# The last pair's second layer as three word passes, with the words made between the groups of the first layer

## The chip, the cores and the metric

One core of one Trainium2 chip runs the kernel. TensorE (PE) multiplies matrices; its weight loads are shown as PEld. VectorE (DVE), ScalarE (ACT) and GpSimd (POOL) do the elementwise work, and SyncE (SP) issues nearly all DMAs. Each engine executes its own instructions in program order and waits for others through semaphores. Here the order of the program is the order in which the Python code emits instructions: the kernel switches the scheduler off (`tc.manual_schedule()`). The metric is the device time of one execution in microseconds (us), as the median of several runs.

## The reference

First a state-space scan (Mamba-2), then a two-layer network with an ELU between its layers. In short:

```python
# attention part: x (4, 8, 768, 32), a (4, 8, 768), B and C (4, 8, 768, 16)
cum = cumsum(log(a))                  # in chunks of tokens
M = (C @ B.T) * exp(cum_i - cum_j) * causal
y = M @ x + (C @ state) * exp(cum)    # and the state is carried on from chunk to chunk
# bridge: y -> 3072 tokens x 256
h = y @ w_in                          # 256 x 2048
g = where(h > 0, h, exp(min(h, 0)) - 1)
out = g @ w_out                       # 2048 x 256
```

All values are float32, and the output has 3072 rows of 256.

## The kernel before

The 3072 tokens are twelve blocks of 256. The blocks 0 and 1 go one by one; from block 2 on they go in pairs (n, n+1), so that n = 2, 4, 6, 8, 10 names a pair of 512 tokens. While the first layer of pair n runs, the scan of pair n + 2 and the second layer of pair n - 2 are threaded in between.

**First layer of a pair.** `l1_words(n, m)` computes one of sixteen groups m of 128 hidden units for 512 tokens. It uses *words*: a float32 number of 24 bits is split exactly into a high and a low word of 12 bits each, in the type `float32r`, which TensorE multiplies in one pass and without error for words this short. With w = w1 + w0 and y = WORD y1 - y0 three products are enough instead of four: `high` = w1 y1 + w0 y0, and `both` = (w0 + w1 / WORD)(y1 - y0); then w y = WORD both + (WORD - 1) high. So each group is three passes of two matmuls of 512 columns (L806), a scaled copy of `both` on ACT (L812), and the sum in place on DVE (L818). `begin_end` follows with two ACT instructions (L824 and L825, the exponential), and `end_words`, called in the middle of the next group, ends the ELU on DVE (L832) and writes the tile `g_of[n, m]`. For even m it also subtracts one half of the tile from the other on POOL (`sub`, L867, called on L836), which the second layer needs.

**Second layer of a pair.** `second(n)` multiplies blocks by the Strassen-Winograd scheme: token blocks, halves of the hidden units and halves of the output columns make a 2 x 2 x 2 product, which seven block products compute instead of eight. They run in two halves of the hidden units, and each product is four steps of two full float32 matmuls of 128 columns (L927). Sums of the weights (`w_sum`, and one quarter of `w_out` overwritten in place, L723), quarters of g that are subtracted from each other on POOL (`sum_t2`, and the calls of `sub` after the products 0 and 1), and additions of the results on DVE (L904, L979) belong to it. `second` is a generator: the loop over groups calls `l2s(count)`, which emits so many of its 56 steps after each group. For the last pair (n = 10) nothing remains to thread it into: `second(n, True)` runs alone at the end (L1376), stores what is complete early and computes its last product in two parts (L907 to L919).

**Buffers.** PSUM has seven buffers in the pool `ps_a` (`high`, `both`, the scan's results and every other product of `second`) and one in `ps_o`. In SBUF, `conv` holds the words of w_in (tag `w64`, eleven buffers) and `ffn` the tiles of g. `raw` and `att` hold what the scan needs; it ends inside the groups of pair 8.

**Order around the change.** The loop `for n in range(4, NP, 2)` (L1327) emits for each of sixteen groups: `l1_words`, a part of the scan's preparation, `begin_end`, the stores of pair n - 4 (at k = 0) and some steps of `second(n - 2)`. The one queue of SP takes the loads of the scan, the stores and, early on, the loads of the weights. `w_out` is ready when POOL has added its last words (L248), before the steps j = 4 and later of the loop on L1196 finish.

Of the kernel before, what the change touches and what calls it, by code (L numbers as in the profile page):

```python
# [10 lines left out]
F32 = mybir.dt.float32  # L11
# [21 lines left out]
def kernel(  # L33
# [38 lines left out]
    assert NG == 3 and MC == 16 and KC == 2 and CW == DM  # L72

    const = ctx.enter_context(tc.tile_pool(name="const", bufs=1))
    raw = ctx.enter_context(tc.tile_pool(name="raw", bufs=3))
    att = ctx.enter_context(tc.tile_pool(name="att", bufs=2))
    ffn = ctx.enter_context(tc.tile_pool(name="ffn", bufs=2))
    conv = ctx.enter_context(tc.tile_pool(name="conv", bufs=2))
    PSUM = bass.MemoryType.PSUM
    p_a = ctx.enter_context(tc.tile_pool(name="ps_a", bufs=7, space=PSUM))  # L80
    p_o = ctx.enter_context(tc.tile_pool(name="ps_o", bufs=1, space=PSUM))
# [647 lines left out]
    w_parts = w_out.rearrange("p (i k) (r c) -> p k r i c", k=2, c=P)  # L729
    a_out = [w_parts[:, k, r] for r in range(2) for k in range(2)]  # L730
    s_out = []

# [60 lines left out]
    def l1_words(n, m, ahead=None):  # L795


        cols = slice(m % 2 * P, (m % 2 + 1) * P)
        w, w0 = k_words[m // 2]
        w1, both_w, w0 = w[:, 0, :, cols], w[:, 1, :, cols], w0[:, :, cols]  # L800
        y1, y0, both_y = y_words[n]
        high, both = psum([P, 2 * BLK], "ps_h"), psum([P, 2 * BLK], "ps_w")
        passes = [(high, w1, y1), (high, w0, y0), (both, both_w, both_y)]
        for ps, lhs, rhs in passes if n > 2 and m == 0 else passes[2:] + passes[:2]:
            for k in range(KC):
                nc.tensor.matmul(  # L806
                    out=ps, lhsT=lhs[:, k], rhs=rhs[:, k], start=k == 0 and lhs is not w0,
                    stop=k == KC - 1 and lhs is not w1)
        if ahead:
            high_of_y(ahead)  # L810
        e = ffn.tile([P, 2 * BLK], F32, tag="e", name="e", bufs=2)
        nc.scalar.activation(e, both, ACT.Copy, scale=WORD)  # L812
        if late:
            end_words()
        if ahead:
            low_of_y(ahead)
            both_of_y(ahead)
        nc.vector.scalar_tensor_tensor(  # L818
            out=high, in0=high, scalar=WORD - 1.0, in1=e, op0=ALU.mult, op1=ALU.add)
        late.append((n, m, high, e))  # L820

    def begin_end():
# [6 lines left out]
    def end_words():  # L829
        n, m, h, e = late.pop(0)  # L830
        g_of[n, m] = ffn.tile([P, 2, BLK], F32, tag=f"g{m % 2}", name="g", bufs=12)
        nc.vector.scalar_tensor_tensor(  # L832
            out=g_of[n, m].rearrange("p b i -> p (b i)"), in0=e, scalar=1.0, in1=h,
            op0=ALU.subtract, op1=ALU.max)
        if m % 2 == 0 and (n, m) != (2, 14):
            sub(g_of[n, m][:, 1], g_of[n, m][:, 1], g_of[n, m][:, 0])  # L836

    def row_of(n):
# [48 lines left out]

    c_of = {}

    def second(n, last=False):  # L890


        c = c_of[n] = ffn.tile([P, 2, 2, 2, P], F32, tag="c", name="c_sum", bufs=1)
        c11, c12, c21, c22 = (c[:, at, :, e] for e in range(2) for at in range(2))
        a11, a12, s1, a22 = a_out
        s2, s3, s4 = s_out
        for half in range(2):
            if not half:
                tmp = ffn.tile([P, 3, 2, P], F32, tag="tmp", name="p_sum", bufs=1)
                p1, p5, u = (tmp[:, r] for r in range(3))  # L900
            chunk = range(4 * half, 4 * half + 4)

            def add(out, in0, in1, eng=nc.vector):
                eng.tensor_tensor(out=out, in0=in0, in1=in1, op=ALU.add)  # L904

            for r, a in enumerate((a11, a12, s1, s2, s3, a22, s4)):
                if last and half and r == 6:  # L907
                    store(n, 0)
                    for ts, queue in enumerate((nc.scalar, nc.sync)):
                        ps = psum([P, P], "ps_o")  # L910
                        for i in chunk:
                            nc.tensor.matmul(
                                out=ps, lhsT=quarters(n, i)[3][:, ts * P:(ts + 1) * P],
                                rhs=a[:, i], start=(i == chunk[0]), stop=(i == chunk[-1]))
                        nc.vector.tensor_tensor(
                            out=c12[:, ts], in0=ps, in1=c12[:, ts], op=ALU.add)
                        r0 = row_of(n + 1) + ts * P
                        queue.dma_start(out=out[r0:r0 + P, 0:P], in_=c12[:, ts])
                    return  # L919
                pool, tag = (p_a, "a") if (7 * half + r) % 2 or n == 2 and not half + r else (  # L920
                    p_o, "o")
                ps = pool.tile([P, 2, P], F32, tag=tag, name="ps_o")
                for i in chunk:
                    b11, b21, b12, b22 = quarters(n, i)
                    b = (b11, b21, b12, t2_of[n, i], b11, b21, b22)[r]
                    for ts in range(2):
                        nc.tensor.matmul(  # L927
                            out=ps[:, ts], lhsT=b[:, ts * P:(ts + 1) * P], rhs=a[:, i],
                            start=(i == chunk[0] and ts == 0), stop=(i == chunk[-1]),
                            skip_group_check=True)  # L930
                    if i < chunk[-1]:
                        yield
                if r == 0:
                    if half:
                        add(p5, ps, c22)
                        add(c21, ps, c21)
                        add(c11, ps, c11)
                    else:
                        nc.scalar.copy(out=p1, in_=ps)  # L939
                    for i in chunk:  # L940
                        b11 = quarters(n, i)[0]
                        sub(b11, t2_of[n, i], b11)
                elif r == 1:
                    add(c11, ps, c11 if half else p1)
                    for i in chunk:
                        b21 = quarters(n, i)[1]
                        sub(b21, b21, t2_of[n, i])
                elif r == 2:
                    add(p5, ps, p5 if half else p1)
                elif r == 3:  # L950
                    add(p5, ps, p5)
                    if half:
                        add(c12, c12, p5, nc.gpsimd)
                        add(c21, ps, c21)
                    else:
                        add(u, ps, p1)
                elif r == 4:
                    if half:
                        add(c21, ps, c21)
                    else:  # L960
                        add(u, ps, u)
                    add(c22, ps, p5)
                    if not half:
                        nc.scalar.copy(out=c12, in_=ps)
                    if last and half:
                        r0 = row_of(n + 1)
                        nc.sync.dma_start(
                            out=out[r0:r0 + BLK, P:2 * P].rearrange("(t p) c -> p t c", p=P),
                            in_=c22)
                    if not half:  # L970
                        sum_t2(n, 1)
                    elif n + 2 < NP:
                        sum_t2(n + 2, 0)
                elif r == 5:
                    add(c21, ps, c21 if half else u)
                elif half:
                    add(c12, ps, c12)
                else:
                    nc.vector.tensor_tensor(out=c12, in0=ps, in1=c12, op=ALU.subtract)  # L979
                yield  # L980

    def store(n, at):
        r0 = row_of(n + at)
# [212 lines left out]
    for j in range(2 * DIRECT):  # L1196
# [35 lines left out]
        if j == 4:  # L1232
            words_of_y(2)
            w_take(15, nc.vector)
            w_give(15)
        if j == 5:
            words_of_w(4)
            both_of_y(2)
# [88 lines left out]
    for n in range(4, NP, 2):  # L1327
# [6 lines left out]

        if n == 4:
            l2s(2)
        for k in range(16):
            l1_words(n, k, m if k == 15 else None)
            turn_step(n, k // 2 * 2 + 1, k % 2)
            if n == 4 and k == 0:  # L1340
                decay(6, 1)
            if n == 4 and 1 < k < 5:
                for _ in range(2):
                    next(left)()
# [5 lines left out]
                store(n - 4, 1)  # L1350
            if not m:
                l2s(4 if k % 2 else 3)
                continue
            l2s((3 - (n == 4), 3 - (n == 4), 3, 3, 3, 3, 3, 3, 4, 5, 2, 2, 3, 1, 3, 0)[k])
            if k == 9:
# [13 lines left out]
                inside(y, m, m + 1, t=1)  # L1369
        if m:  # L1370
            l2s(4)
        end_words()
        for _ in steps:
            pass
    n = NP - 2
    for k, _ in enumerate(second(n, True)):  # L1376
        if k == 0:
            store(n - 2, 0)
            store(n - 2, 1)


# [28 lines left out]
```

## Time and profile before

| | |
|---|---|
| median of 3 runs | 350.15 us (349.76 to 350.74) |
| span of the profiled execution | 347.9 us (the page gives no other time of that execution) |
| PE busy | 340.7 us (98%) |
| DVE, ACT, POOL busy | 258.4, 234.1, 218.0 us |
| chain that ended last | PE 63%, DVE 11%, ACT 10%, POOL 7% |
| granted TensorE clock | 0.999 of full speed |
| DMA in the slices of the last third | 0 to 1 tenths, 2 tenths in the last slice |

The span runs from the first to the last instruction of the program; the runs' times are longer by what lies around it. The chain is followed back from the last instruction: each piece is what the next one waited for. A timeline line gives the start, the duration, the engine, the line of the code, the operation, output and inputs, the shape, and how many instructions were merged; in brackets it has the idle time before it and who ended it. Matmuls overlap in such lines, so the price of one is the distance between starts. A full float32 matmul appears as two records.

### The profile page before, as it was taken

The numbers are of one execution on the slowest core, as the hardware profiler recorded it, in microseconds if no ns is written. First come the engines' busy times: TensorE is split into PE (matmuls) and PEld (weight loads), VectorE is DVE, ScalarE is ACT, GpSimd is POOL, SyncE is SP. The second block draws the span as 40 slices with busy tenths as digits, with TensorE's granted clock in tenths as the row PEclk, the third lists the DMA queues.
The fourth block names the chain that finished last, engine by engine and source line by source line (L and its number), as shares of the span: only waits on it lengthen the run. The fifth ranks groups of instructions, "written<-read, shape, count | busy, mean of one in ns | idle before, by whom it ended". The sixth has DMA issues, their size and how long they took to land.

```text
span 347.9 us, 9991 instructions
## 1 busy us (share of the span) xinstructions
PE 340.7 (98%) x3934; PEld 299.3 (86%) x3934; DVE 258.4 (74%) x515; ACT 234.1 (67%) x537; POOL 218.0 (63%) x338
## 2 busy tenths in 40 slices
PE   8899999999999999999999999999999999999996
PEld 6579888888788889889889888889988989999996
DVE  3998989889997899876788766778776756665232
ACT  4789989598658988457699457599557366565000
POOL 5654554539999799965296765196855174455760
PEclk9999999999999999999999999999999999999999
DMA  8989969381360610260421160320000100001002
GB/s 144 258 204 220 273 130 266 81 150 44 66 138 2 135 38 12 34 137 4 117 51 30 17 154 4 95 44 0 2 2 5 60 2 1 0 2 55 9 2 62
DMA packets 72728, 26.51 MB, mean 76 GB/s; under 512 B 57768, under 2 KB 67560, under 8 KB 72680
## 3 DMA queue, kind: packets, MB, share of 16 engines
q1 hardware_dynamic: 70360, 25.60, 31.7%
q8 instruction: 31, 0.51, 0.6%
q10 hardware_dynamic: 2320, 0.26, 0.5%
q14 instruction: 17, 0.14, 0.1%
HBM read 22.51 MB, written 3.34 MB: 74 GB/s over the span
## 4 chain that ended last, share of the span: by engine, by line
PE 63%; DVE 11%; ACT 10%; POOL 7%; issue 4%; SPq 2%; DMA 2%; DVEq 0%; POOLq 0%; ACTq 0%
PE ps_o L927 22%; PE ps_h L806 11%; PE ps_h L676 11%; PE ps_o L851 8%; PE ps_w L806 6%; DVE ps_h L818 3%; ACT e L824 3%; POOL g L867 3%; ACT e L825 2%; DMA w<-in_moe_w_in_dram 2%; POOL t L867 2%; DVE M L559 2%; PE ps_y L643 2%; DVE y L780 2%; POOL w L867 1%
## 5 line engine op out<-in xcount | busy, mean ns | idle before, releaser
L927 PEld LDWEIGHTS ps_o<-w_out,g 128*128 128x128 f32 x640 | 78.7, 191 | 5.4 <-ACT p_sum L939 1.2
L927 PE MATMUL ps_o<-w_out,g 128*128 128x128 f32 x640 | 81.2, 276 | 0.7 <-ACT p_sum L939 0.6
L824 ACT ACTIVATE e<-ps_h 128x512 f32<-128x512 f32 x72 | 43.0, 598 | 56.9 <-DVE ps_h L818 56.9
L832 DVE SCALAR_TENSOR_TENSOR g<-e,ps_h 128x512 f32<-128x512 f32 x72 | 49.4, 686 | 35.0 <-ACT e L825 33.4
L867 POOL TENSOR_TENSOR g<-g 128x256 f32<-128x256 f32 x36 | 28.6, 794 | 58.2 <-DVE g L832 58.2
L818 DVE SCALAR_TENSOR_TENSOR ps_h<-ps_h,e 128x512 f32<-128x512 f32 x72 | 50.0, 694 | 11.2 <-ACT e L812 9.0
L806 PE MATMUL ps_w<-y_both,w_words 128*128 128x512 f32 x144 | 51.5, 437 | 0.1
L812 ACT ACTIVATE e<-ps_w 128x512 f32<-128x512 f32 x72 | 42.2, 586 | 11.1 <-PE ps_w L806 11.0
L825 ACT ACTIVATE e<-e 128x512 f32<-128x512 f32 x72 | 45.5, 631 | 2.3
L676 PE MATMUL ps_h<-yT,w_in 128*128 128x256 f32 (+1 forms) x208 | 45.1, 367 | 1.9 <-ACT w_in L205 1.1
L806 PE MATMUL ps_h<-y,w_words 128*128 128x512 f32 x144 | 45.5, 398 | 0.0
L806 PE MATMUL ps_h<-y,w 128*128 128x512 f32 x144 | 44.9, 392 | 0.0
L676 PEld LDWEIGHTS ps_h<-yT,w_in 128*128 128x128 f32 x208 | 36.4, 190 | 7.5 <-POOL w_in L248 2.6
L530 ACT ACTIVATE L<-L,ncum 128x64 f32<-128x64 f32 x160 | 42.2, 337 | 0.1
L927 PE MATMUL ps_o<-w_sum,g 128*128 128x128 f32 x304 | 38.6, 276 | 0.0
L927 PEld LDWEIGHTS ps_o<-w_sum,g 128*128 128x128 f32 x304 | 37.0, 192 | 1.4
L535 POOL TENSOR_SCALAR_AFFINE_SELECT L<-L 64x512 f32<-64x512 f32 x40 | 29.4, 735 | 8.0 <-ACT L L530 6.7
L806 PEld LDWEIGHTS ps_h<-y,w 128*128 128x128 f32 x144 | 27.0, 188 | 6.9 <-POOL w L867 0.4
L806 PEld LDWEIGHTS ps_h<-y,w_words 128*128 128x128 f32 x144 | 26.6, 188 | 6.2 <-issue 0.5
L867 POOL TENSOR_TENSOR g<-t,g 128x256 f32<-128x256 f32 x40 | 28.1, 736 | 5.8 <-PE ps_o L927 5.7
L851 PE MATMUL ps_o<-w_out,g 128*128 128x256 f32 x128 | 30.4, 381 | 0.0
L867 POOL TENSOR_TENSOR g<-g,t 128x256 f32<-128x256 f32 x40 | 28.7, 748 | 0.2
(135 smaller groups left out, 537.5 us busy)
## 6 DMA issues: line engine op xcount, KB each, us to landing
L<-flat SPq DMA_DIRECT2D x20, 256.0 KB
w<-in_moe_w_out_dram SPq DMA_DIRECT2D x8, 512.0 KB
w<-in_moe_w_in_dram SPq DMA_DIRECT2D x7, 512.0 KB
xr<-in_x_dram SPq DMA_DIRECT2D x24, 128.0 KB
out_dram<-c_sum SPq DMA_DIRECT2D x9, 256.0 KB
bc<-in_B_dram SPq DMA_DIRECT2D x24, 64.0 KB
bc<-in_C_dram SPq DMA_DIRECT2D x22, 64.0 KB
ec<-flat_exp SPq DMA_DIRECT2D x10, 128.0 KB
```

The costliest lines, as they stand in the source:

```text
L530: nc.scalar.activation(L[:, h, u], L[:, h, u], ACT.Exp, bias=ncum[:, u, row:row + 1])
L535: nc.gpsimd.affine_select(out=part, in_=part, pattern=[[0, 4], [0, 2], [1, Q]], compare_op=ALU.is_ge, fill=0.0, base=0, channel_multiplier=-1)
L676: nc.tensor.matmul(out=ps[:, j, toks], lhsT=w_in[i][:, k, j * P:(j + 1) * P], rhs=yT[n // 2][:, k, n % 2].rearrange("p u i -> p (u i)")[:, ...
L806: nc.tensor.matmul(out=ps, lhsT=lhs[:, k], rhs=rhs[:, k], start=k == 0 and lhs is not w0, stop=k == KC - 1 and lhs is not w1)
L812: nc.scalar.activation(e, both, ACT.Copy, scale=WORD)
L818: nc.vector.scalar_tensor_tensor(out=high, in0=high, scalar=WORD - 1.0, in1=e, op0=ALU.mult, op1=ALU.add)
L824: nc.scalar.activation(e, high, ACT.Relu, scale=-1.0)
L825: nc.scalar.activation(e, e, ACT.Exp, scale=-1.0)
L832: nc.vector.scalar_tensor_tensor(out=g_of[n, m].rearrange("p b i -> p (b i)"), in0=e, scalar=1.0, in1=h, op0=ALU.subtract, op1=ALU.max)
L851: nc.tensor.matmul(out=o_of[n][:, ts], lhsT=g_of[n, j][:, m % 2, ts * P:(ts + 1) * P], rhs=w_out[:, m], start=(m == 0 and ts == 0), stop=( ...
L867: nc.gpsimd.tensor_tensor(out=out, in0=in0, in1=in1, op=ALU.subtract)
L927: nc.tensor.matmul(out=ps[:, ts], lhsT=b[:, ts * P:(ts + 1) * P], rhs=a[:, i], start=(i == chunk[0] and ts == 0), stop=(i == chunk[-1]), s ...
```

## The change

The second layer of the last pair no longer uses the seven block products. It is computed as sixteen contractions over 128 hidden units, for four blocks of 128 tokens, each in three word passes of 256 columns.

- `w_out` has to be had unchanged, since the scheme of the other pairs overwrites a quarter of it. `keep_w` copies its four quarters to a DRAM tile `w_kept`, one at j = 4 of the early loop, and three among the groups of n = 4.
- After the groups of n = 8 `late_pool` closes the pools of the scan and opens a pool in their place. Four DMAs bring the weights back, and buffers for their words are made.
- The words are *jobs*: eight for two slices of the weights each, sixteen for the tiles of g. A job has three steps: the high word on ACT, a second word on DVE, a third on POOL. From the third group of n = 10 on, `first_of_job` puts one ACT step behind the copy of `both`, `second_of_job` one DVE step behind L818, and `third_of_job` one POOL step behind the steps of `second(8)`, each for another job, so that a job passes through three groups. Jobs that are left (one of the weights, the last nine of g and the rest of those begun) go on beside the new second layer, and there the third step of g's words is on DVE too.
- `late_l2(m, t)` issues the three matmuls of slice m and token block t, `late_out` the copy on ACT, the sum on DVE and the store of a block. The first twelve slices go over all four token blocks each; the last four slices go block by block, so that the blocks end one after the other. The fourth block's `high` has its own PSUM bank.
- What the seven products needed goes: the subtractions of `end_words` and `sum_t2` for the last pair, and the special end of `second`.

```diff
-    def second(n, last=False):
+    def second(n):
...
-                if last and half and r == 6:
...
-                    elif n + 2 < NP:
+                    elif n + 4 < NP:
                         sum_t2(n + 2, 0)
...
+    def keep_w(k, r):
+        nc.sync.dma_start(out=kept_parts[:, k, r], in_=w_parts[:, k, r])
...
         nc.scalar.activation(e, both, ACT.Copy, scale=WORD)
+        if n == NP - 2 and m > 1:
+            first_of_job()
...
             out=high, in0=high, scalar=WORD - 1.0, in1=e, op0=ALU.mult, op1=ALU.add)
+        if n == NP - 2 and m > 1:
+            second_of_job()
...
-        if m % 2 == 0 and (n, m) != (2, 14):
+        if m % 2 == 0 and (n, m) != (2, 14) and n < NP - 2:
             sub(g_of[n, m][:, 1], g_of[n, m][:, 1], g_of[n, m][:, 0])
...
+    def late_words_of_w(i):
+        w, w1, both = late_w[i]
+        yield nc.scalar.activation(w1, w, ACT.Copy, scale=NEAR)
+        yield nc.vector.scalar_tensor_tensor(
+            out=both, in0=w1.bitcast(F32), scalar=1.0 / WORD - 1.0, in1=w,
+            op0=ALU.mult, op1=ALU.add)
+        yield sub(w.bitcast(F32R), w, w1.bitcast(F32))
+
+    def late_words_of_g(n, m):
...
+        yield nc.scalar.activation(words[:, 0], g, ACT.Copy, scale=NEAR / WORD)
+        yield nc.vector.scalar_tensor_tensor(
+            out=low, in0=words[:, 0].bitcast(F32), scalar=WORD, in1=g,
+            op0=ALU.mult, op1=ALU.subtract)
+        if alone:
+            yield nc.vector.scalar_tensor_tensor(
+                out=words[:, 1], in0=words[:, 0].bitcast(F32), scalar=1.0 - WORD, in1=g,
+                op0=ALU.mult, op1=ALU.add)
+        else:
+            yield sub(words[:, 1], words[:, 0].bitcast(F32), low.bitcast(F32))
...
+    def late_l2(m, t):
+
+        g1, g0, both_g = (g[:, t * P:(t + 1) * P] for g in late_g[m])
+        w0, w1, both_w = (w[:, m % 2] for w in late_w[m // 2])
...
+        if m == 0:
+            both = psum([P, 2, DM], "ps_both")
+            total.append((both[:, 0], psum([P, DM], "ps_high") if t == 3 else both[:, 1]))
+        both, high = total[t]
+        for ps, lhs, rhs in ((both, both_g, both_w), (high, g1, w1), (high, g0, w0)):
+            nc.tensor.matmul(
+                out=ps, lhsT=lhs, rhs=rhs,
...
+    def late_out(n, t):
+        both, high = total[t]
+        e = ffn.tile([P, DM], F32, tag="t2", name="e_out", bufs=4)
+        nc.scalar.activation(e, both, ACT.Copy, scale=WORD)
+        o = ffn.tile([P, DM], F32, tag="t2", name="o_out", bufs=4)
+        nc.vector.scalar_tensor_tensor(
+            out=o, in0=high, scalar=WORD - 1.0, in1=e, op0=ALU.mult, op1=ALU.add)
+        r0 = row_of(n + t // 2) + t % 2 * P
+        nc.sync.dma_start(out=out[r0:r0 + P, :], in_=o)
...
+            if n == 4 and k in (3, 5, 7):
+                keep_w(int(k > 3), int(k > 5))
...
                 l2s(4 if k % 2 else 3)
+                third_of_job()
                 continue
...
+        if m == NP - 2:
+            late_pool()
...
-    for k, _ in enumerate(second(n, True)):
-        if k == 0:
-            store(n - 2, 0)
-            store(n - 2, 1)
+    store(n - 2, 0)
+    store(n - 2, 1)
+    alone.append(True)
+    for m in range(MC - 4):
+        first_of_job()
+        second_of_job()
+        third_of_job()
+        for t in range(4):
+            late_l2(m, t)
+    for t in range(4):
+        for m in range(MC - 4, MC):
+            late_l2(m, t)
+        late_out(n, t)
```

## The prediction

> **What bounds the kernel now.** I read the page first: busy time, then the chain that ended last.
>
> ```profile
> PE 340.7 (98%) x3934; PEld 299.3 (86%) x3934; DVE 258.4 (74%) x515; ACT 234.1 (67%) x537; POOL 218.0 (63%) x338
> ...
> PE 63%; DVE 11%; ACT 10%; POOL 7%; issue 4%; SPq 2%; DMA 2%; DVEq 0%; POOLq 0%; ACTq 0%
> ```
>
> TensorE (PE) is busy 98%, and no other engine comes close. The chain in order of time then shows the stage that the change replaces:
>
> ```profile
> 317.95 25.01 PE ps_o L927 x224
> 342.96 1.80 PE ps_o L912 x16
> 344.76 0.02 issue
> 344.79 0.29 DVE c_sum L915
> ```
>
> At the end PE alone sets the time. These are 240 records of 0.1117 us. The first 16 belong to the pair before (its last product), so the last pair's second layer starts at 317.95 + 16 x 0.1117 = 319.74 and takes 224 x 0.1117 = 25.02, to 344.76. After that come 3.15 us of adding, storing and landing, to 347.91.
>
> What one matmul costs is read from PE's timeline, as the distance from start to start (the printed durations overlap):
>
> ```profile
> 107.49 0.62 PE L806 MATMUL ps_h<-y,w 128*128 128x512 f32 x2
> 107.95 0.62 PE L806 MATMUL ps_w<-y_both,w_words 128*128 128x512 f32 x2
> 108.41 0.62 PE L806 MATMUL ps_h<-y,w_words 128*128 128x512 f32 x2
> 108.86 0.61 PE L806 MATMUL ps_h<-y,w 128*128 128x512 f32 x2
> 109.31 3.61 PE L851 MATMUL ps_o<-w_out,g 128*128 128x256 f32 x16
> 112.76 1.05 PE L927 MATMUL ps_o<-w_out,g 128*128 128x128 f32 x8
> ...
> 319.57 5.52 PE L927 MATMUL ps_o<-w_out,g 128*128 128x128 f32 x48
> 324.93 1.95 PE L927 MATMUL ps_o<-w_sum,t 128*128 128x128 f32 x16
> ```
>
> A full f32 product is two records: 256 columns cost (112.76 - 109.31) / 16 = 0.216 per record, 128 columns (324.93 - 319.57) / 48 = 0.1117. A word product (L806) is one record: 512 columns in 0.45 to 0.47 per two, so 0.227 to 0.235 each.
>
> Last, the first layer's groups, where the new work is put. One group of the last pair, ScalarE (ACT) and VectorE (DVE):
>
> ```profile
> 305.44 0.58 ACT L812 ACTIVATE e<-ps_w 128x512 f32<-128x512 f32 x1
> 306.99 0.60 ACT L824 ACTIVATE e<-ps_h 128x512 f32<-128x512 f32 x1 [0.97 <-DVE ps_h L818]
> ...
> 306.26 0.70 DVE L818 SCALAR_TENSOR_TENSOR ps_h<-ps_h,e 128x512 f32<-128x512 f32 x1
> 307.08 0.42 DVE L904 TENSOR_TENSOR p_sum<-ps_o,p_sum 128x256 f32<-128x256 f32 x1
> 308.36 0.69 DVE L832 SCALAR_TENSOR_TENSOR g<-e,ps_h 128x512 f32<-128x512 f32 x1 [0.85 <-ACT e L825]
> 309.42 0.70 DVE L818 SCALAR_TENSOR_TENSOR ps_h<-ps_h,e 128x512 f32<-128x512 f32 x1 [0.38 <-PE ps_h L806]
> ```
>
> ACT waits 0.97 for L818, DVE 0.85 for the exponential and 0.38 for PE: here lies the free time that the words must fit into. A group lasts 2.7 (three steps of the layer before) or 3.2 us (four), 2.95 on average.
>
> **The last stage on PE.** Removed: 224 records, 25.02 us. Added: 16 x 4 x 3 = 192 word products of 256 columns. No row has that shape with words. Lower end: each needs a new 128x128 weight load, and the shortest step with one, 128 columns of f32, takes 0.112. Half of the 512-column word step is 0.116. If a word step shrinks with its columns as the f32 record does (0.216 to 0.1117), it is 0.231 x 0.517 = 0.120. If what a word step has above the f32 record, 0.231 - 0.216 = 0.015, is paid per instruction, it is 0.108 + 0.015 = 0.123. Upper end: if load and stream shared one read rate, (512 + 128) columns in 0.231 make (256 + 128) take 0.139. I take 0.120, the reading that rests on a measured halving: 192 x 0.120 = 23.0 us, a gain of 2.0 (3.5 at 0.112, a loss of 1.7 at 0.139).
>
> The Trainium skill (TensorE: Matmul & The Clock Gate, Back-to-back issue gap) gives N/2.4 + 2.5 ns for a warm matmul. For 512 columns that is 215.8; the word rows do not agree (227 to 235). By it the 192 would take an estimated 21.0 us.
>
> **The tail.** Now PE's end is followed by an add of 0.29 on 128x128 and a 64 KB store. Then: an ACT copy of 128x256 (0.37, row L939), whose input is complete two matmuls before PE ends, so 0.24 of it is covered; a VectorE operation on 128x256 (0.42, row L904); a 128 KB store. VectorE ends 0.05 + 0.37 - 0.24 + 0.42 = 0.6 after PE instead of 0.33: +0.27. A 256 KB store's packets of 1 KB take about 1.0 us, so 128 KB about 0.4 to 0.5 against 0.34: +0.1. Together +0.35 (0.2 to 0.8). The last copy also reuses the buffer of the first of the four stores, which by then has some 3 us, against 2.4 from issue to span end now: covered, by little.
>
> **Words in the first layer's groups.** From the third group on, one job each: an ACT copy (0.6), a VectorE operation on 128x512, and two groups after the copy a POOL subtraction of 128x512 (two rows of 0.735: 1.47). ACT: 0.6 goes into the wait of 0.97. POOL: the last pair's own subtractions go (8 of 0.74 in `end_words`, 4 after L972); some 12 x 1.47 = 18 come, beside 20 x 0.735 that stay, in 44 us. The t2, b11 and b21 quarters stand in the same queue; a subtraction ahead of them delays them by 1.5 to 4 us, and after the ninth group PE needs them 9 to 12 us later. Nothing. VectorE is the doubtful one: L818 and L832 start to start 0.61 each, 19 adds over 16 groups of 0.34 = 0.40, so 1.62 before; the job adds 0.61 alone, or more when POOL is reading:
>
> ```profile
> L780 DVE SCALAR_TENSOR_TENSOR y<-y,yT x10: 684/689/1216, 75.0 to 269.8; 128x512 fp32r<-128x512 f32 x10
> ...
> 269.35 1.11 POOL L867 TENSOR_TENSOR g<-g 128x256 f32<-128x256 f32 x1 [3.03 <-DVE g L832]
> ```
>
> With two SBUF inputs VectorE took 1.216 beside a POOL subtraction, 0.684 without; POOL took 1.11 instead of 0.735. L818 and L832 (one input in PSUM) never exceed 0.70. So 2.2 to 2.85 us per group, under 2.95. What lags is caught by PSUM: seven buffers at some 2.44 per group leave PE about 4 us. What can come out is the last `high` tile, which the fourth token block's sums take over: PE reaches it 9 matmuls (1.1 us) into the stage, and L832 has freed it 320.88 - 319.74 = 1.14 after the start now. I charge 0.3 (0 to 2.7, the rival below).
>
> The Trainium skill (SBUF — State Buffer, section SBUF: two separate sides) has this as an exclusive lock for the whole instruction, the loser blocked. The 1.216 agrees; by it a job behind a 1.47 us subtraction could last an estimated 2.1, and the sum would be the VectorE rival's.
>
> **The rest, charged nothing.** VectorE words after the first layer: 21 operations of 0.61 = 12.8 us beside 12 x 12 x 0.120 = 17.3 us of PE, no POOL behind them: the last one has 3 us in hand. The copy of the weights to DRAM (4 x 512 KB): the first DMA waits on SP for POOL's L248, which ends at 79.5; SP's next, a store at 83.5, is not held, and the first overwrite on POOL (L723, 92.7) comes 13 us later. The other three stand on SP ahead of loads needed a stage later. Lower end 0, upper end 0.6, one DMA issue on SP. The reload (4 x 512 KB) waits on SP for the scan's last product (264.3); at 200 to 270 GB/s (the page's slices) it is in by 275, before the third group (277). Behind it on SP stand the stores of the pair before, issued at 273.2 as now; VectorE first overwrites that tile at 281.1. If the reload took 16 us instead, VectorE would wait about 2 us, inside PE's 4.
>
> **Sum.** 347.91 - 25.02 + 23.04 + 0.35 + 0.3 = 346.6 us of span, 1.3 less. The page gives no time of the profiled execution beyond its span; the runs' median lies 2.24 above it (350.15), which I take as unchanged: 348.8 us.
>
> **Rivals.**
> Weights as the only limit (faster): steps of 0.112. For it: f32 rows with as many loads run at 0.112; against it: every word step exceeds the f32 record of the same page by 0.011 to 0.019. 21.5 us, so 347.3; the skill's rule would land beside it.
> Load and stream share a rate (slower): steps of 0.139, 26.7 us: 352.5; from 0.127 on nothing is gained. For it: the word rows' excess; against it: f32 loads and streams overlap without loss.
> VectorE falls behind in the groups (slower): from 1.35 us per job on, L818 to L818 is 0.61 + 0.61 + 1.35 + 0.40 > 2.95; at 1.55 the 14 jobs leave 14 x 0.2 = 2.8 us of lag, which the fourth token block's sums wait for, nearly whole: +2.7 - 0.3, so 351.2. For it: the 1.216 row and a POOL busy three quarters of the time; against it: 1.1 us of slack per group.
> The words do not run as one pass at 256 columns: two records of 0.112 to 0.120, some 44.5 us for the stage: 370. Against it: L806 has one record per product.
>
> **How the numbers follow.** My forecast (steps of 0.114 to 0.128, little lag; 347.6 to 350.3) has 0.52; weights only 0.17; shared rate 0.11; VectorE behind 0.17; two passes 0.03. No change that a measurement of this kernel can tell is within 0.3%, 1.05 us. Faster: 0.30 of the forecast plus 0.17: 0.47. Same: 0.22 of it plus 0.05 of a small lag: 0.27. Slower: 0.26. The range 347.0 to 351.8 takes in 0.112 below and a full VectorE lag above; it leaves out the shared rate, two passes and a little below, some 0.18.
>
> **What would show it.** Starts of the 256-column word matmuls: 0.120 right; 0.112 or 0.139 name the rivals. PE's idle time at the fourth token block of the first step: 0.3. VectorE's jobs in the groups: 0.7 to 1.2, and L818 still every 2.95. From PE's last end to the span's end: 3.5. I am wrong if PE idles in the last pair's groups or the step is above 0.130.

## The result, and the profile after

The changed kernel took 348.74 us (348.37 to 349.17) against 350.15 us (349.76 to 350.74): a ratio of 0.9957 (95% interval 0.9945 to 0.9969), 1.4 us (0.4%) faster, and the whole interval lies below 1. The forecast was 348.8.

The page of the changed kernel, busy time and the chain that ended last:

```profile
PE 339.5 (98%) x3902; PEld 297.7 (86%) x3902; DVE 275.3 (79%) x533; ACT 247.7 (71%) x563; POOL 215.8 (62%) x319
...
PE 61%; DVE 12%; ACT 11%; POOL 5%; issue 5%; SPq 2%; DMA 2%; DVEq 0%; ACTq 0%; POOLq 0%
```

PE has 32 records fewer (192 in place of 224). VectorE has 17 us more work and ScalarE 14, and PE is still the engine that sets the end. The chain of the changed kernel in order of time, last groups and last stage:

```profile
318.63 1.78 PE ps_o L924 x16
320.41 1.19 PE ps_both L1042 x10
321.60 0.24 PE ps_high L1042 x2
...
337.68 4.44 PE ps_both L1042 x37
...
343.08 0.13 PE ps_both L1042
343.22 0.02 issue
343.24 0.39 ACT e_out L1050
343.63 0.02 issue
343.66 0.42 DVE o_out L1052
```

The last stage begins at 320.41 and has no piece but PE's until the last copy; with the two matmuls that still run beside that copy it ends at 320.41 + 192 x 0.120 = 343.45. The step itself, from PE's timeline (the distance from start to start counts, the durations overlap):

```profile
322.40 0.28 PE L1042 MATMUL ps_both<-w_both,g_words 128*128 128x256 f32 x1
322.52 0.28 PE L1042 MATMUL ps_both<-w_high,g_words 128*128 128x256 f32 x1
322.64 0.28 PE L1042 MATMUL ps_both<-w_again,g_low 128*128 128x256 f32 x1
```

One record for each word product, 0.120 apart. So the stage takes 23.04 us where the seven products took 25.02.

The groups ahead of it: busy time of the engines while the words are made, before and after (columns: window, length, then busy time with the number of instructions for PE, PEld, DVE, ACT and POOL, the granted clock, DMA share and GB/s). Before:

```profile
282.00:320.00 38.00, 38.00 (x263) 34.80 (x262) 24.31 (x44) 23.58 (x41) 19.09 (x28) 1.00 0.03 8
```

After:

```profile
282.00:320.00 38.00, 38.00 (x260) 34.67 (x259) 33.65 (x57) 30.22 (x54) 27.04 (x25) 1.00 0.03 8
```

Net of what went, VectorE has 9.3 us more, ScalarE 6.6 and POOL 8.0, and PE's 38.00 us of work in 38.00 stay as they were.

Where did the time go? The last product of the scan comes before anything of the new stage in both kernels; the last of its 64 records starts at 264.05 before and 264.74 after (the first at 263.41 and 264.10). From there on I count the rest:

| us | before | after | difference |
|---|---|---|---|
| start of the last record of the scan's last product | 264.05 | 264.74 | +0.69 |
| from there to the start of PE's last matmul | 80.42 | 78.42 | -2.00 |
| from there to the end of the span | 3.44 | 3.83 | +0.39 |
| span | 347.91 | 346.99 | -0.92 |

I take the first row as scatter: it arises in the first 26 us, where the two programs do the same, and stays between 0.67 and 0.73 from there to the scan's end. In the ten other profiled executions below (two of the changed kernel, eight of kernels with the same program until then) that point lies between 263.86 and 265.49. The kernel before has only one profile, but its spans beside the experiments go from 347.6 to 349.3, so it scatters too. Without that row the change is worth -2.00 + 0.39 = -1.6 us in this pair of executions, and -1.4 in the medians.

### The profile page after: what moved, and what is told of

The parts are those of the page before. It is cut to its first block, busy times and chain, and to the rows that moved or that the text cites. A ratio compares the mean times of both kernels' runs of the same rounds, so it can differ in the third digit from the quotient of the medians.

```text
span 347.0 us, 9962 instructions
## 1 busy us (share of the span) xinstructions
PE 339.5 (98%) x3902; PEld 297.7 (86%) x3902; DVE 275.3 (79%) x533; ACT 247.7 (71%) x563; POOL 215.8 (62%) x319
## 4 chain that ended last, share of the span: by engine, by line
PE 61%; DVE 12%; ACT 11%; POOL 5%; issue 5%; SPq 2%; DMA 2%; DVEq 0%; ACTq 0%; POOLq 0%
PE ps_o L924 16%; PE ps_h L812 11%; PE ps_h L677 11%; PE ps_o L861 6%; PE ps_w L812 6%; PE ps_both L1042 6%; DVE ps_h L826 4%; ACT e L834 4%; POOL g L877 3%; ACT e L835 3%; DVE y L786 2%; DMA w<-in_moe_w_in_dram 2%; ACT yT L661 2%; DVE M L560 2%; DVE y_both L796 1%
## 5 line engine op out<-in xcount | busy, mean ns | idle before, releaser
L834 ACT ACTIVATE e<-ps_h 128x512 f32<-128x512 f32 x72 | 43.0, 598 | 49.0 <-DVE ps_h L826 49.0
L924 PEld LDWEIGHTS ps_o<-w_out,g 128*128 128x128 f32 x512 | 64.1, 191 | 5.3 <-ACT p_sum L936 1.1
L924 PE MATMUL ps_o<-w_out,g 128*128 128x128 f32 x512 | 66.3, 276 | 0.6 <-ACT p_sum L936 0.4
L818 ACT ACTIVATE e<-ps_w 128x512 f32<-128x512 f32 x72 | 42.2, 586 | 10.8 <-PE ps_w L812 10.6
L877 POOL TENSOR_TENSOR g<-g 128x256 f32<-128x256 f32 x28 | 22.7, 811 | 36.2 <-DVE g L842 36.1
L924 PE MATMUL ps_o<-w_sum,g 128*128 128x128 f32 x256 | 32.8, 276 | 0.0
L924 PEld LDWEIGHTS ps_o<-w_sum,g 128*128 128x128 f32 x256 | 31.4, 191 | 1.4
L861 PEld LDWEIGHTS ps_o<-w_out,g 128*128 128x128 f32 x128 | 24.0, 190 | 3.5
L877 POOL TENSOR_TENSOR g<-t,g 128x256 f32<-128x256 f32 x32 | 23.1, 750 | 4.7 <-PE ps_o L924 4.7
```

Of the source, the lines that this page charges most:

```text
L834: nc.scalar.activation(e, high, ACT.Relu, scale=-1.0)
L861: nc.tensor.matmul(out=o_of[n][:, ts], lhsT=g_of[n, j][:, m % 2, ts * P:(ts + 1) * P], rhs=w_out[:, m], start=(m == 0 and ts == 0), stop=( ...
L877: nc.gpsimd.tensor_tensor(out=out, in0=in0, in1=in1, op=ALU.subtract)
L924: nc.tensor.matmul(out=ps[:, ts], lhsT=b[:, ts * P:(ts + 1) * P], rhs=a[:, i], start=(i == chunk[0] and ts == 0), stop=(i == chunk[-1]), s ...
```

## The experiments

All the diffs are against the changed kernel. "Groups" is the time from the last record of the scan's last product to the end of the pair before's last product, 55.51 us in the changed kernel; "stage" is what follows up to the end of PE's last matmul.

**The changed kernel once more**, beside the next three runs.

> The changed kernel once more, beside the runs that follow. Both theories expect what was measured: 0.996 of before, 348.7 us. In the profile: 192 word matmuls 0.120 apart, 23.0 us from the first to the end of the last, and 3.5 us from there to the span's end. The changed kernel's profile started its last stage 0.67 us later than that of before, and that shift is already there at 26 us, where both programs are the same; if it is chance of the loads at the start, it is another number here.

348.71 us (348.54 to 348.93), ratio 0.9967 (0.9956 to 0.9979). Groups 55.51, stage 23.04. A third time, beside the last experiments:

> The changed kernel beside the combination, on the same chip: 348.5 to 348.9 us, stage 23.04, groups 55.51 from the scan's last product to the end of the groups.

348.49 us (347.39 to 349.73), ratio 0.9957 (0.9939 to 0.9974); groups 55.54, stage 23.03. What scatters is the start: the stretch from the scan to PE's last matmul was 78.42, 78.43 and 78.45 in the three.

**No words at all in the groups and beside the stage.** The jobs and the reload are left out, and the stage multiplies words of `w_in` that lie there in place of the right ones: the making of the words is what this kernel lacks.

```diff
-                jobs += [late_words_of_w(i), late_words_of_g(n, i)]
-            jobs += [late_words_of_g(n, i) for i in range(MC // 2, MC)]
+                pass
...
-        if m == NP - 2:
-            late_pool()
```

> No words are made and no weights are reloaded: the 192 matmuls of the last stage take words of the first layer's weights that lie in SBUF as both operands, so the last pair's output is not the product of the second layer. The copies of the weights to DRAM stay. If the jobs are covered by PE, as the prediction charged (0.3 at most, 0 in the profile), the time equals the changed kernel's within 0.3 us: 0.995 to 0.996. If VectorE, ScalarE or POOL hold PE up anywhere in the groups or in the last stage, the time falls by that much: the VectorE rival would have it 2.4 us lower, 0.989.

348.19 us (347.70 to 349.34), ratio 0.9956 (0.9942 to 0.9970). Groups 55.53, stage 23.04, from the scan to PE's last matmul 78.44: the same as with the words. VectorE was busy for 24.88 us in the window where it had 33.65 with the jobs. So the whole making of the words, the reload and the waits that they add cost PE nothing. The median is 0.5 below the changed kernel's beside it, but the six runs scatter over 1.6 us, and PE's stretch, which the start does not touch, is the same.

**VectorE's steps of the jobs twice.** Inside the groups every VectorE step is issued a second time; beside the last stage all stays.

```diff
-        yield nc.vector.scalar_tensor_tensor(
-            out=both, ...)
+        for _ in range(1 if alone else 2):
+            nc.vector.scalar_tensor_tensor(
+                out=both, ...)
+        yield
```

(and the same for `low` in `late_words_of_g`)

> VectorE makes the second word of each of the 14 jobs in the groups twice (same result), not beside the last stage. In the changed kernel's profile a job's VectorE step takes 0.68 to 1.71, 0.93 on average, and VectorE has 2.5 of 2.95 us per group. With 0.6 to 0.9 more it needs 3.1 to 3.4, falls behind by 0.2 to 0.4 per group and is 3 to 5 us late at the end. By the prediction's account PSUM covers about 4 us for PE inside the groups, and the lag comes out where the last stage takes over the last `high` tile: 1.5 to 4 us longer, 1.000 to 1.008 of before. If VectorE has more room than I count, the time stays at 0.996; if its lag reaches PE at once, PE idles in the groups and the time is 4 to 8 us longer.

355.42 us, ratio 1.0151 (1.0127 to 1.0176). Groups 62.25 (+6.74), stage 23.04. PE's waits and the chain of this kernel, at the place where PE stood still:

```profile
PE ps_o L924 <- DVE c_sum L914: 4.9, 1, 4.9
```

```profile
306.63 0.41 DVE p_sum L914
307.04 0.66 DVE c_sum L914 x2
307.70 0.59 DVE g L842
308.30 0.61 DVE ps_h L826
308.90 0.99 DVE g_low L1009
...
311.48 0.42 DVE c_sum L914
311.90 0.14 issue
312.04 1.98 PE ps_o L924 x8
```

It is the last case of the expectation: the lag reaches PE inside the groups, in one stop of 4.9 us. PE wants the only buffer `ps_o` for the next product of the pair before, and the addition that frees it (L914) stands on VectorE behind a group's sums and two words. VectorE was busy for 41.66 of the 44 us from 282 to 326. But 4.9 is not 6.7. The last line of the chain shows what follows: eight f32 records in 1.98 us, 0.25 each instead of 0.112. The windows around the stop (PE's busy time, then the other engines', then the granted clock):

```profile
306.00:312.00 6.00, 1.14 (x10) 0.91 (x8) 5.97 (x10) 2.91 (x6) 5.30 (x7) 1.00 0.00 0
312.00:313.00 1.00, 0.96 (x5) 0.99 (x6) 1.00 (x2) 0.00 (x0) 0.97 (x1) 0.56 0.00 0
313.00:314.00 1.00, 1.00 (x6) 1.00 (x6) 0.97 (x3) 0.84 (x2) 0.00 (x0) 0.50 0.06 16
314.00:315.00 1.00, 1.00 (x4) 0.81 (x3) 1.00 (x3) 0.48 (x2) 0.00 (x0) 0.50 0.00 0
315.00:316.00 1.00, 1.00 (x5) 0.72 (x4) 0.34 (x1) 1.00 (x2) 0.00 (x0) 0.74 0.00 0
316.00:317.00 1.00, 1.00 (x11) 1.00 (x9) 0.73 (x2) 0.03 (x1) 0.00 (x0) 1.00 0.00 0
```

After the stop TensorE's granted clock was 0.5 for some 3.5 us. The chain has 8 f32 records, 2 and 4 words there (8 x 0.112 + 6 x 0.231 = 2.28 us) from 312.04 to 316.16, 4.12 us: 1.84 lost, and 4.9 + 1.84 = 6.7, the whole of it. Counted from start to start against the changed kernel, where a stop has its slow first step in it, the stop is 5.07 and the slow steps behind it are 1.68; so some 1.7 us go to the clock. The Trainium skill (TensorE: Matmul & The Clock Gate, Part 1: The HAM clock gate) has the clock fall to one half after an idle window of about 3.4 us and come back after as much activity; the rows agree, with half the clock for some 3.5 us after a stop of 4.9.

**The same with the single buffer out of the way.** Doubled steps again, and all the products of the second half of the pair n = 8 go to the seven buffers.

```diff
-                pool, tag = (p_a, "a") if (7 * half + r) % 2 or n == 2 and not half + r else (
+                pool, tag = (p_a, "a") if (7 * half + r) % 2 or n == 2 and not half + r or n == NP - 4 and half else (
```

> VectorE's steps of the jobs in the groups are issued twice, as in the run before, and the products of the second half of the pair n = 8 now all go to the seven buffers instead of every other one to the single buffer. Theory A: PE stopped for 4.9 us at 306.9 only because every other product needs the one buffer ps_o, which VectorE's late addition held; with seven buffers the stop goes or shrinks below 2 us, and what is left of the lag shows as waits of L812 or at the start of the last stage; the time is 349 to 353 us. Theory B: VectorE is simply full (41.66 us busy of 44), and the place where it stops PE doesn't matter: the groups still end 5.5 to 7 us later than without the doubled steps, through other waits, and the time stays at 354 to 356 us. I lean to B, since only 2.3 us of VectorE's time were idle in that stretch.

353.98 us, ratio 1.0114 (1.0100 to 1.0129). Groups 59.57 (+4.06), stage 24.39 (+1.35). PE's waits in this kernel:

```profile
PE ps_h L812 <- ACT e L818: 3.2, 3, 1.2
...
PE ps_both L1046 <- ACT e L818: 1.1, 1, 1.1
```

The stop at `ps_o` is gone and turns into three short waits of the first layer and one in the last stage, six matmuls after its start, where the third token block takes over the bank of the last `both`. The copy L818 that frees it, at 325.11, stands on ScalarE behind L834, and L834 has waited for VectorE's sum:

```profile
323.94 0.60 ACT L834 ACTIVATE e<-ps_h 128x512 f32<-128x512 f32 x1 [2.38 <-DVE ps_h L826]
```

That the waits would move there was theory A's; that moving them would not help was B's, and the time lies at B's lower edge: 4.06 + 1.35 = 5.4 us are lost in waiting, where the one stop was 5.1 by the same count. VectorE is simply full. What the run did gain, 1.3 to 1.4 us, is the clock: none of these waits lasts over 1.5 us, and the granted clock stayed at 1.00 (windows with PE's busy time, then the clock):

```profile
305.00:314.00 9.00, 6.87 (x42) 1.00 0.01 2
314.00:324.00 10.00, 8.94 (x62) 1.00 0.00 0
324.00:327.00 3.00, 1.91 (x16) 1.00 0.17 58
```

So the single buffer's harm was to gather the waits into one stop that was long enough to halve the clock. No theory of mine had that in it.

**The late words on POOL.** Beside the last stage the third step of g's words goes to POOL, as in the groups.

```diff
-        if alone:
+        if False:
```

> The part of the change called late ones on VectorE undone: beside the last stage the third word of a tile of g is made by POOL, as in the groups. Then each of the twelve slices has 0.6 of VectorE and 1.3 of POOL, which hinder each other if both read SBUF with two inputs (in the profiles 1.2 to 1.7 instead of 0.68 for VectorE). If they exclude each other for a whole instruction, a slice takes 1.3 + 0.68 = 2.0 against 1.44 on PE: the eight or nine jobs left end about 18 to 20 us after the stage's start, PE wants the last of them at 17.3 and waits 1 to 3 us: 0.998 to 1.004 of before. If they share without exclusion, or the slack of six slices is enough, the time stays at 0.996.

350.11 us, ratio 0.9999 (0.9984 to 1.0014): the whole gain is gone. Stage 24.99 (+1.95), groups as before. VectorE's and POOL's timelines and the chain in this kernel:

```profile
322.93 15.39 DVE L1006 SCALAR_TENSOR_TENSOR g_low<-g_words,g 128x512 fp32r<-128x512 f32 x9
```

```profile
325.83 14.85 POOL L877 TENSOR_TENSOR g_words<-g_words,g_low 128x512 fp32r<-128x512 f32 x9
```

```profile
327.54 11.91 POOL g_words L877 x7
339.44 1.24 POOLq L1499
340.69 0.04 issue
340.73 3.62 PE ps_both L1042 x28
```

Nine operations of VectorE and nine of POOL, and each engine ends one every 11.91 / 7 = 1.70 us (14.85 / 9 = 1.65 with the last one, which has VectorE no longer beside it). That is more than the 1.44 us that PE takes for a slice, so the words fall behind, and PE waits for POOL's last two, 0.8 and 0.6 us. It is the first case of the expectation, with 1.7 in place of 2.0 for a slice. In the changed kernel VectorE does both of a tile's words in 2 x 0.60:

```profile
326.17 0.68 DVE L1006 SCALAR_TENSOR_TENSOR g_low<-g_words,g 128x512 fp32r<-128x512 f32 x1
326.77 0.68 DVE L1010 SCALAR_TENSOR_TENSOR g_words<-g_words,g 128x512 fp32r<-128x512 f32 x1
...
334.00 1.28 DVE L1010 SCALAR_TENSOR_TENSOR g_words<-g_words,g 128x512 fp32r<-128x512 f32 x2
```

It is done at 335.28; the last tile's words are first needed after 337.7. So making the late words on VectorE alone is a necessary part of the change.

**A job in one group instead of three.**

```diff
-        if len(once) > 1 or once and not jobs:
+        if once:
...
-        if len(twice) > 1 or twice and not once:
+        if twice:
```

> The spreading over three groups undone: the three steps of a job are issued in one and the same group. VectorE's step then waits for the ACT step of its own group (ACT is done with it 0.5 to 0.6 after the copy of `both`, about when L826 ends), POOL's for VectorE's. ACT's step ends before L826 in the profile, so VectorE should wait for nothing new, and POOL has the end of the group: by PE's account the time stays within 0.3 us of the changed kernel, 0.995 to 0.997. If the spreading is what keeps the queues apart, VectorE waits in each of 14 groups, L826 lags and the time is 1 to 4 us longer.

348.38 us, ratio 0.9944 (0.9927 to 0.9962). Groups 55.51, stage 23.04. VectorE waits for nothing new, as expected; POOL waits 5.9 and 4.7 us in all for VectorE's words of w and g in the groups, and none of it reaches PE. The spreading over three groups is not needed in this kernel.

**Narrower last slices.** In the last four slices the token blocks 1, 2 and 3 are multiplied in 192, 128 and 64 columns only; the rest of those sums is left out.

```diff
+        cols = slice(0, DM - 64 * t if m >= MC - 4 else DM)
...
-                out=ps, lhsT=lhs, rhs=rhs,
+                out=ps[:, cols], lhsT=lhs, rhs=rhs[:, cols],
```

> In the last four slices the token blocks use 256, 192, 128 and 64 columns of the weights' words instead of 256 (the columns left out lack these slices in the output). Twelve matmuls in a row of each width. If the 0.120 is the stream of columns above a floor set by the weight load, 256 columns give 0.120 and the rest about 0.112, the step of the f32 rows with a load each. If 0.120 is itself the price of loading words, all four widths give 0.120. If only columns count, 0.120, 0.090, 0.060, 0.030.

One run, 348.46 us; only its steps are read. PE's timeline of this kernel, one place for each width:

```profile
338.56 0.28 PE L1043 MATMUL ps_both<-w_both,g_words 128*128 128x256 f32 x1
338.68 0.28 PE L1043 MATMUL ps_both<-w_high,g_words 128*128 128x256 f32 x1
...
339.34 0.27 PE L1043 MATMUL ps_both<-w_high,g_words 128*128 128x192 f32 x1
339.45 0.28 PE L1043 MATMUL ps_both<-w_again,g_low 128*128 128x192 f32 x1
...
340.65 0.27 PE L1043 MATMUL ps_both<-w_high,g_words 128*128 128x128 f32 x1
340.76 0.27 PE L1043 MATMUL ps_both<-w_again,g_low 128*128 128x128 f32 x1
...
342.30 0.28 PE L1043 MATMUL ps_high<-w_high,g_words 128*128 128x64 f32 x1
342.41 0.28 PE L1043 MATMUL ps_high<-w_again,g_low 128*128 128x64 f32 x1
```

0.120 at 256 columns; 0.111 to 0.112 at 192, 128 and 64 alike. There is a floor, the same as for the f32 records of 128 columns, and the step at 256 columns lies above it: the first of the three cases.

**The tail split.** In the fourth token block all passes of `both` come first, so that ScalarE's copy has eight matmuls to hide behind, and the last sum and store go in two halves over two queues.

```diff
-        for m in range(MC - 4, MC):
-            late_l2(m, t)
+        for passes in ((0,), (1, 2)) if t == 3 else ((0, 1, 2),):
+            for m in range(MC - 4, MC):
+                late_l2(m, t, passes)
```

> Only the end of the fourth token block differs: its four `both` matmuls of the last slices come before the eight `high` ones, so that the copy on ACT is done before PE ends, and the sum and the store go in two halves of 128 columns over two queues, as the kernel before did. If the tail's price is the chain copy, sum, larger store, as the prediction has it (+0.38 in the profile), PE's end to the span's end goes from 3.53 back to about 3.2 and the time falls by 0.3 us to 0.995 of before. If the longer tail came from something else (the four stores in a row, the landing), it stays at 3.5 and 0.996.

348.60 us, ratio 0.9963 (0.9951 to 0.9976). The last sums of this kernel on VectorE, and the last one of the changed kernel in the run beside it:

```profile
343.30 0.49 DVE L1056 SCALAR_TENSOR_TENSOR o_out<-ps_high,e_out 128x128 f32<-128x128 f32 x2 [0.65 <-PE ps_high L1043]
```

```profile
343.41 0.42 DVE L1052 SCALAR_TENSOR_TENSOR o_out<-ps_high,e_out 128x256 f32<-128x256 f32 x1 [0.78 <-ACT e_out L1050]
```

The wait is now for PE and no longer for ScalarE, yet from the start of PE's last matmul VectorE's end comes only 0.06 earlier, after 0.86 instead of 0.92 us: the first half starts 0.12 earlier, and two halves take 0.49 instead of 0.42. The end of the span did not come nearer to PE's end (3.89 from the start of the last matmul, against 3.84). The tail's price is only in small part the copy.

**Both together**, the job in one group and the split tail.

> The jobs' steps all in one group, and the last block's end split in two halves, both together. If the two runs of the single edits (348.38 and 348.60) each hold a real gain over the changed kernel (348.71), this gives 348.2 to 348.4; if they only show the scatter of the start, 348.5 to 348.9, the same as the changed kernel beside it. Stage 23.04 and groups 55.5 in both cases.

348.38 us (348.12 to 348.86), ratio 0.9955 (0.9943 to 0.9967), beside 348.49 and 0.9957 for the changed kernel: not to be told apart. Groups 55.52, stage 23.04. No version found here beats the changed kernel beyond the scatter.

## Why the prediction was right

**What bounds the kernel.** Right: PE alone, in the stage and in the groups ahead of it. The run without words shows it most directly, since the same 78.4 us of PE are left when the words are gone.

**The last stage on PE, 192 x 0.120 = 23.0.** Right to 0.04 us: step 0.120, stage 23.04, 25.02 before. The reading from the halving of the f32 record held. The rivals for the step are out: weights alone would be 0.112, which exists as a floor but only up to 192 columns; a shared rate would be 0.139; two passes would be two records. By the rule of the Trainium skill (TensorE: Matmul & The Clock Gate, Back-to-back issue gap) for an isolated warm matmul, N/2.4 + 2.5 ns, 256 columns would take an estimated 109.2 ns; the trace has 120, and 111 to 112 for narrower words, in a stream where each matmul has a weight load.

**The tail, +0.35 (0.2 to 0.8).** The first part was right: VectorE ends 344.08 - 343.45 = 0.63 after PE, where I said 0.6, and 0.32 before. The second, +0.1 for the larger store, is in the packets of the last store (0.51 us for 128 KB, 0.41 for 64 KB before), but the rest of that way was 0.3 shorter: from VectorE's end to PE's closing instruction, which comes after the stores have landed, it took 2.08 to 2.10 us after and 2.30 before. Instead there was something that I had not thought of: the program's last instructions, two semaphore events on GpSimd, lie 0.37 us apart in some executions and 0.08 in others. From the start of PE's last matmul to the end of the span it took 3.44 before, and 3.83, 3.84 and 3.84 in three executions of the changed kernel, but 3.54 with the job in one group and with the late words on POOL, where nothing of the tail is changed, and 3.58 in the last combination. So the tail costs +0.1 or +0.4, depending on those 0.3 us; that +0.35 came out right in size is luck. Why the end varies is open: all three executions of the changed kernel had the long distance, so it need not be chance.

**VectorE in the groups, +0.3 (0 to 2.7).** The size was within its bounds, the value 0. The price of the words was as put: 0.68 alone and up to 1.71 beside POOL, 0.91 in the mean of the thirteen that fell into the groups. VectorE's 33.65 us in 38.00 make 2.6 per group of 2.95, within the estimate of 2.2 to 2.85. VectorE's timeline of the changed kernel:

```profile
289.84 1.71 DVE L995 SCALAR_TENSOR_TENSOR w_both<-w_high,w_again 128x512 fp32r<-128x512 f32 x1
...
293.80 0.68 DVE L1006 SCALAR_TENSOR_TENSOR g_low<-g_words,g 128x512 fp32r<-128x512 f32 x1
...
307.54 1.42 DVE L995 SCALAR_TENSOR_TENSOR w_both<-w_high,w_again 128x512 fp32r<-128x512 f32 x1
```

POOL's 128x512 subtractions lasted 1.26 to 1.30, and four of them 1.68 to 1.76 (I had 1.47). What failed is the account of where a lag would come out, and its price. I had it caught by seven buffers, 4 us, until the fourth token block. With doubled steps it came out earlier, at the single buffer of every other product, and with that out of the way at the first layer's banks and the third token block. And the rival "VectorE falls behind" was priced by the lag alone; one stop of 4.9 us cost some 1.7 more through the clock. The rival was a real one, with its threshold somewhere between single and double work.

**POOL, the copies and the reload, charged nothing.** Right. PE waited for POOL nowhere in the last pair's groups, and the reload (issued from 265.1 on) and the stores behind it made nobody wait that reached PE; without them the groups took 55.53 us. The copies of the weights to DRAM stayed in that run, but all four lie before the scan's end, up to which the shift between both kernels is constant within 0.06 us. **The words beside the last stage, charged nothing because 12.8 us lie beside 17.3 of PE.** Right, and the run on POOL is the counter-test: with 1.70 us per tile in place of 1.20 the cover is gone and the stage 1.95 us longer. VectorE's late words ended 335.28 - 320.41 = 14.9 us into the stage and not 12.8, since work of the first layer, and one word that took 1.79 us beside POOL, came in between.

**The sum.** By terms, foretold -1.98 + 0.35 + 0.3 = -1.3 of span; measured -2.00 + 0.39 + 0, and +0.69 of a later start, which no term can hold. The median was 0.06 from the forecast, which is luck with a start that scatters over 1.6 us.

## What to carry to other kernels

Where PE is the bound, price a rewritten stage by its number of matmuls and the start-to-start step of the nearest shape on the same page, scaled by columns, with the floor for short ones in mind. Work added to an engine off the path is free until that engine is full, so add up its busy time in the very window, with the prices that it has beside the neighbour it shares memory with; when it falls behind, the waits are lost wherever they lie, but here four of 0.9 to 1.2 us were cheaper than one of 4.9 us, after which TensorE's clock was halved for some 3.5 us. To compare two profiled executions, anchor both at the last point that the change can't touch: here the spans differ by 0.9 us, and from the anchor on by 1.6.

## What the runs showed of the hardware that I had not expected

- One stop of TensorE of 4.9 us cost 6.7: the granted clock was 0.50 to 0.56 for the next 3 us. Stops of 0.9 to 1.2 us, three within 10 us, left it at 1.00. No stop between these sizes stands in the last pair's groups or stage of any run.
- The word matmul has a floor of 0.111 to 0.112 us, at 192 columns as at 64. Since each of them loads a 128x128 tile of weights, the load is the likely cause; no run here separates it from another fixed cost.
- From 256 to 512 columns a word step grows from 0.120 to 0.227 to 0.235, by 0.42 to 0.45 ns for each column.
- VectorE and POOL with both inputs in SBUF held each other up for 15 us, nine operations each. A pair took 1.70 us; start to start alone they take 0.60 and, by two subtractions in a row (307.14 and 308.38), 1.24, together 1.84. So they hardly run side by side: 0.14 of the sum is saved. The Trainium skill (SBUF — State Buffer, SBUF: two separate sides) has an exclusive lock for a whole instruction; the period agrees nearly, and the records themselves, which overlap, cannot show the turns.
- The packets of a final store of 128 KB took 0.51 us, those of one of 64 KB 0.39 (split tail) and 0.41 (before); from VectorE's end to the closing instruction it was 2.1, 2.2 and 2.3 us, so the size of the last store does not decide that way.
- The program's start scatters by up to 1.6 us at the scan's end, and its end by 0.3 us, between kernels that are the same there. The split of the tail was to gain 0.3.
